# A causal convolution before a gated feed-forward layer: convolution lanes that divide one flat row of chunks and tokens

## The chip, the cores and the metric

One core of a Trainium2 chip runs the whole kernel. The metric is the device time of one execution in microseconds. Its engines run side by side, each with a queue of its own: TensorE (PE, with its weight loads shown as PEld), VectorE (DVE), ScalarE (ACT), GpSimd (POOL) and SyncE (SP, which here only issues DMAs). An instruction waits for another engine on semaphores.

## The reference: what is computed

`x` is (8, 4096, 192): 8 sequences of 4096 tokens, 192 channels in 8 heads of 24. A softmax over 7 taps per head gives the weights of a causal convolution along the tokens; its output goes through a feed-forward layer with a ReLU gate.

```python
w = softmax(weight, axis=-1)                  # (8 heads, 7 taps)
x_pad = concatenate([zeros(B, 6, D), x], axis=1)
conv[b, s, h, g] = sum_k w[h, k] * x_pad[b, s + k, h, g]
xc = conv.reshape(32768, 192)
gate = maximum(xc @ moe_w_gate, 0.0)          # 192 -> 1536
val = xc @ moe_w_val
out = (gate * val) @ moe_w_out                # 1536 -> 192
```

## The kernel before, in words

**Units.** The work is cut into 16 units (`NUNIT`) of 1024 tokens (`UNIT`), each for a pair of sequences at once: `bp` and `bp + 4` are the two streams. A partition holds one channel of one stream: 64 channels of stream 0 on partitions 0 to 63, the same of stream 1 on 64 to 127. The 192 channels make three chunks (`NCH` = 3), so the convolved input of a unit, `xc[u]`, is a tile of 128 partitions x 3 chunks x 1024 tokens.

**Gate phase.** `gate_val(u, w)` (two windows `w` of 512 tokens, 12 blocks `f` of 128 hidden channels each) does 12 matmuls per block into two PSUM tiles (line 450), six for the gate and six for the value; ScalarE takes the ReLU of the gate (line 459), and DVE multiplies it with the value, read straight from PSUM (line 460), into `hT`. PSUM has four tiles `ps`, handed out in turn to everything.

**Projection.** After both windows, three calls of `project_columns(hs, p)` (line 470, 96 matmuls each) make 64 output columns each in a `ps` tile, and `turn_out` (line 484, DVE) transposes each into the output tile. The next unit's gate phase needs the same PSUM tiles: its first gate tile, first value tile and second gate tile are free early, and its second value tile is the one that the third `turn_out` of the unit before releases. `store` then puts four DMAs on SP.

**Convolution lanes.** The first two units are convolved by TensorE (`conv_dense`, `conv`). For all later units `u + 2`, the convolution is done by the other engines while unit `u` is in its projection:

- `lane_load` (GpSimd) loads `x` as `x_e`, tokens on partitions; `lane_turn` copies it on GpSimd into `x_p` (line 375) and turns it by DMA transposes on SP (line 378) into `x_r`, channels on partitions, tokens along the row. `x_r` has nine blocks of 128 (`TILES`): four for DVE's tokens and five for the others', each part with its own 64 tokens of halo ahead of it.
- Of every chunk, DVE has the first 448 tokens (`LDVE`), ScalarE and GpSimd the last 576 (`LPOOL`).
- DVE's part: ScalarE makes tap 0 (`lane_first`, line 416, three instructions), and DVE adds taps 1 to 6 by `scalar_tensor_tensor` (`lane_rest`, line 427): 18 instructions, one per tap and chunk. `STEPS` says how many of them are issued ahead of each of the three `turn_out`s: 5, 6 and 7.
- The other part: ScalarE makes the products of taps 0 to 4 in fp32 (`product`, line 396, 15 instructions), in the order of `TAPS`: taps 1 and 2 in the first third of the projection, 3 and 4 in the second, 0 in the last. GpSimd sums them with `add` (line 405): `prod0 += prod1`, then 2, and so on; taps 5 and 6 (`ON_POOL`) it multiplies itself first (line 398). The last `add` writes `xc`.

**Order on GpSimd.** In the loop over `u`, GpSimd's queue holds `add(u+1, 1)`, `lane_turn(u+2)` and `lane_load(u+3)`, the adds of taps 2 to 5, and the add of tap 6, which is written behind the gate phase in the code but waits for nothing in it. For u = 1 the load and two adds come ahead of `lane_turn`; from u = 13 on there is no load, and at u = 14 no `lane_turn`. Each product tile, `prod0` to `prod6`, has one buffer: a product of the next unit waits until the add that reads that tile is done. `x_r` has two buffers. Nothing is reordered by a planner: the order of each queue is the order in the code.

Of the kernel before, what the change touches and what calls it, by code (L numbers as in the profile page):

```python
# [8 lines left out]
FP = mybir.dt.float32  # L9
F16 = mybir.dt.float16  # L10
ACTF = mybir.ActivationFunctionType
ALU = mybir.AluOpType
# [3 lines left out]
def kernel(  # L16
# [12 lines left out]
    nc = tc.nc  # L29

    B, S, D = x.shape
    H, KW = weight.shape
# [3 lines left out]
    NB = B // 2  # L36
    NCH = D // 64
# [2 lines left out]
    WIN = 512  # L40
    NWIN = S // WIN
    SUB = 112
    ON_POOL = (5, 6)
    STEPS = [5, 6, 7]
    TAPS = [(1, 2), (3, 4), (0,)]
    GSUB = 5


    UNIT = 2 * WIN
    NUNIT = NB * S // UNIT  # L50
    HALO = 64
    LDVE, LPOOL = 448, 576
    TILES = (UNIT + 2 * HALO) // 128
    TDVE = (LDVE + HALO) // 128
    GROUPS = [(0, [WIN * w + SUB * j for j in range(GSUB)]) for w in range(2)]
    second = [min(t, 2 * UNIT - SUB) for t in range(UNIT, 2 * UNIT, SUB)]
    GROUPS += [(0, second[:GSUB]), (0, second[GSUB:])]
# [2 lines left out]
    const = ctx.enter_context(tc.tile_pool(name="const", bufs=1))  # L60
    epool = ctx.enter_context(tc.tile_pool(name="epool", bufs=1))
    rpool = ctx.enter_context(tc.tile_pool(name="rpool", bufs=2))
    apool = ctx.enter_context(tc.tile_pool(name="apool", bufs=1))
# [48 lines left out]
    for half, eng in ((0, nc.sync), (1, nc.scalar)):  # L112
        eng.dma_start(
            out=wr[64 * half : 64 * half + 64],
            in_=bass.AP(
                tensor=weight.tensor,
                offset=weight.offset + 2 * half * HQ * KW,
                ap=[[HQ * KW, 2], [0, 32], [1, HQ * KW]],
            ),
# [79 lines left out]
    tap = const.tile([128, NCH, KW], FP)  # L199

    def load_taps():
# [19 lines left out]
    prod = const.tile([128, HQ, BW, KW], FP)  # L221
# [12 lines left out]
    for q in range(4):  # L234
        for j in range(4):
            s0 = 32 * j - PAD
            lo, hi = max(0, -s0), min(BW, SUB - s0)
# [12 lines left out]
    xc = {}  # L250
# [91 lines left out]
    xes, xrs, accs, prods = {}, {}, {}, {}  # L342

    def lane_load(u):


        bp, t0 = u * UNIT // S, u * UNIT % S
        xe = epool.tile([128, TILES, 2, NCH, 64], F16, name="x_e")
        j0 = int(t0 == 0)
        if j0:  # L350
            nc.gpsimd.memset(xe[0:HALO, 0, :, :, :], 0.0)
        for st in range(2):
            b = bp + NB * st
            for j, n in ((j0, TDVE - j0), (TDVE, TILES - TDVE)):
                lo = t0 - HALO + 128 * j if j < TDVE else t0 + LDVE - HALO
                nc.gpsimd.dma_start(  # L356
                    out=xe[:, j : j + n, st, :, :].rearrange("p j c r -> p j (c r)"),
                    in_=bass.AP(
                        tensor=x.tensor,
                        offset=x.offset + (b * S + lo) * D,  # L360
                        ap=[[D, 128], [128 * D, n], [1, D]],
                    ),
                )
            if j0:
                nc.gpsimd.dma_start(
                    out=xe[HALO:128, 0, st, :, :].rearrange("p c r -> p (c r)"),
                    in_=x[b, 0 : 128 - HALO, :],
                )
        xes[u] = xe

    def lane_turn(u):
        xe = xes.pop(u)
        xp = epool.tile([128, TILES, NCH, 2, 64], F16, name="x_p")
        for st in range(2):
            nc.gpsimd.tensor_copy(out=xp[:, :, :, st, :], in_=xe[:, :, st, :, :])  # L375
        xr = rpool.tile([128, NCH, 128 * TILES], F16, name="x_r")
        for j in range(TILES):
            nc.sync.dma_start_transpose(
                out=xr[:, :, 128 * j : 128 * j + 128],
                in_=xp[:, j].rearrange("p c s r -> p (c s r)"),  # L380
            )
        xrs[u] = xr

    def shifted(u, c, k, lane):
        o = HALO - KW + 1 + k
        if lane:
            return xrs[u][:, c, 128 * TDVE + o : 128 * TDVE + o + LPOOL]
        return xrs[u][:, c, o : o + LDVE]

    def product(engine, u, c, k):  # L390
        if (u, k) not in prods:
            prods[u, k] = apool.tile([128, NCH, LPOOL], FP, name=f"prod{k}")
        out = prods[u, k][:, c, :]
        in_, scale = shifted(u, c, k, 1), tap[:, c, k : k + 1]
        if engine is nc.scalar:
            engine.activation(out=out, in_=in_, func=ACTF.Copy, scale=scale)  # L396
        else:
            engine.tensor_scalar(out=out, in0=in_, scalar1=scale, scalar2=None, op0=ALU.mult)  # L398

    def add(u, k):  # L400
        if k in ON_POOL:
            for c in range(NCH):
                product(nc.gpsimd, u, c, k)
        p0 = prods[u, 0]
        nc.gpsimd.tensor_tensor(  # L405
            out=p0[:] if k < KW - 1 else xc[u][:, :, LDVE:UNIT],
            in0=p0[:],
            in1=prods.pop((u, k))[:],
            op=ALU.add,
        )  # L410

    def lane_first(u):
        accs[u] = apool.tile([128, NCH, LDVE], FP, name="acc")
        xc[u] = xcpool.tile([128, NCH, UNIT], F16, name="xc")
        for c in range(NCH):
            nc.scalar.activation(  # L416
                out=accs[u][:, c, :],
                in_=shifted(u, c, 0, 0),
                func=ACTF.Copy,
                scale=tap[:, c, 0:1],  # L420
            )

    def lane_rest(u):
        acc = accs.pop(u)
        for k in range(1, KW):
            for c in range(NCH):
                nc.vector.scalar_tensor_tensor(  # L427
                    out=xc[u][:, c, 0:LDVE] if k == KW - 1 else acc[:, c, :],
                    in0=shifted(u, c, k, 0),
                    scalar=tap[:, c, k : k + 1],  # L430
                    in1=acc[:, c, :],
                    op0=ALU.mult,
                    op1=ALU.add,
                )
                yield
# [45 lines left out]
    def turn_out(ps, o, p):  # L481


        nc.vector.transpose(  # L484
            out=o[:, :, 64 * p : 64 * p + 64].rearrange("p t (b c) -> p b t c", b=2),
            in_=ps[:].rearrange("p b (t c) -> p b t c", c=32),
        )

    def store(o, bp, w0):
        for s in range(4):  # L490
            row0 = (bp + NB * (s % 2)) * S + WIN * (w0 + s // 2)
            nc.sync.dma_start(
                out=out[row0 : row0 + WIN, :].rearrange("(t p) d -> p t d", p=32),
                in_=o[32 * s : 32 * s + 32],
            )
# [33 lines left out]
    for u in range(NUNIT):  # L529
        lane = 1 <= u < NUNIT - 1  # L530
        if lane:
            add(u + 1, 1)
        if u == 1:
            lane_load(3)
            add(2, 2)
            add(2, 3)
        if u + 2 < NUNIT:
            lane_turn(u + 2)
        if u == 0:
            xts[3] = load_x(3)  # L540
# [12 lines left out]
        bp, w0 = u * UNIT // S, u * UNIT % S // WIN  # L553
        lane = None
        if u + 2 < NUNIT:
            lane_first(u + 2)
            lane = lane_rest(u + 2)
        o = opool.tile([128, UNIT // 64, D], FP, name="out_s")
        if u == NUNIT - 1:
            for i in range(4):  # L560
                project(bp, w0 + i // 2, hs[i // 2], i % 2, i == 3, o[:, 4 * i : 4 * i + 4, :])
            continue
        for p in range(3):
            ps = project_columns(hs, p)
            if lane:
                for k in TAPS[p]:
                    for c in range(NCH):
                        product(nc.scalar, u + 2, c, k)
                for _ in range(STEPS[p]):
                    next(lane)  # L570
            turn_out(ps, o, p)
            if u == 0 and p == 0:
                conv(3)
        store(o, bp, w0)
# [30 lines left out]
```

## Time and profile before

| | |
|---|---|
| Median of 3 runs | 903.69 us (902.73 to 904.63) |
| The profiled execution | 903.87 us, of which the span is 902.2 us |
| PE busy / idle ahead of line 450's value matmuls | 789.6 us / 105.4 us |
| DVE busy | 792.2 us: gate products (line 460) 468.3, lanes (line 427) 214.8 + 50.9, transposes (line 484) 56.1 |
| ACT busy | 568.9 us: ReLU (line 459) 393.2, products (line 396) 141.4, first tap (line 416) 24.9 |
| POOL busy | 597.4 us: adds (line 405) 271.7 + 53.8, products (line 398) 144.3, copies (line 375) 54.3 |
| Granted TensorE clock, mean | 0.934 of full |

Rows of the groups read: line, engine, operation, output<-inputs, shapes, count | busy us, mean ns of one | idle time of the engine just ahead of them, and who ended most of it. Rows of the timeline read: start in us from the span's start, duration in us, engine, line, what, count of merged neighbours, and in brackets the idle time ahead and who ended it; a merged row lasts from its first start to its last end. Matmuls overlap, so a row of six lasts a little longer than the distance to the next row.

### The profile page before, as it was taken

The page shows a single profiled execution, that of the slowest core. Times are in us where ns is not written, and L with a number is a line of the kernel's source. Part 1 is how long each engine was busy: PE and PEld are TensorE (multiplying, and loading weights), DVE is VectorE, ACT ScalarE, POOL GpSimd, SP SyncE. Part 2 cuts the span into 40 slices and gives each one's busy share as a digit, 9 for nine tenths or more (in the row PEclk, how much of TensorE's full clock was granted, in tenths as well). Part 3 has the DMA queues.
Part 4 walks back from the last instruction along what each step waited for, and adds up shares of the span by engine and source line. Part 5 has one row for each costly group of instructions (what it writes and reads, how often), then busy time and mean ns, then how long its engine had stood idle before and what let it go on. Part 6 is the DMA issues. An engine that isn't in the chain of part 4 may idle for free.

```text
span 902.2 us, 21815 instructions
## 1 busy us (share of the span) xinstructions
PE 789.6 (88%) x9392; PEld 402.2 (45%) x9392; DVE 792.2 (88%) x711; ACT 568.9 (63%) x663; POOL 597.4 (66%) x299
## 2 busy tenths in 40 slices
PE   8996979989797997979979798897979929939998
PEld 4543535435353453535435354453535415415447
DVE  7888999989899898998989899898998998989492
ACT  5784847758376684847758477583856807717272
POOL 9429769495894949769396794949849396293000
PEclk9997989989899898989989899898999969969999
DMA  9929434070520707125060340806217004020122
GB/s 113 127 49 143 45 51 100 2 138 13 103 48 4 145 3 121 30 28 123 3 130 20 61 88 1 145 7 110 42 12 140 1 15 96 2 57 14 25 48 71
DMA packets 132580, 55.80 MB, mean 62 GB/s; under 512 B 98180, under 2 KB 132484, under 8 KB 132484
## 3 DMA queue, kind: packets, MB, share of 16 engines
q1 hardware_dynamic: 90466, 38.35, 19.4%
q0 software_dynamic: 41808, 15.97, 16.1%
q8 instruction: 73, 1.20, 0.6%
q14 instruction: 23, 0.19, 0.1%
q10 hardware_dynamic: 210, 0.10, 0.0%
HBM read 31.93 MB, written 25.17 MB: 63 GB/s over the span
## 4 chain that ended last, share of the span: by engine, by line
PE 75%; DVE 19%; issue 4%; DMA 0%; ACT 0%; DVEq 0%
PE ps L450 55%; PE ps L470 18%; DVE acc L427 11%; DVE xc L427 4%; DVE out_s L484 4%; PE ps L506 2%; DMA wr<-in_weight_dram 0%; DVE hT L460 0%; ACT gr L459 0%; PE ps L305 0%; PE ps L280 0%; DVE band L243 0%; DVE prod L224 0%; DVE blk L232 0%; ACT out_s L517 0%
## 5 line engine op out<-in xcount | busy, mean ns | idle before, releaser
L459 ACT ACTIVATE gr<-ps 128x1024 f16<-128x1024 f32 x384 | 393.2, 1024 | 309.8 <-PE ps L450 309.8
L460 DVE TENSOR_TENSOR hT<-gr,ps 128x1024 f16<-128x1024 f16 x384 | 468.3, 1220 | 59.7 <-PE ps L450 26.4
L450 PE MATMUL ps<-xc,Wv 64*128 64x512 f16 x2304 | 334.4, 393 | 105.4 <-DVE out_s L484 103.9
L405 POOL TENSOR_TENSOR prod<-prod,prod 128x1728 f32<-128x1728 f32 x70 | 271.7, 3881 | 212.1 <-ACT prod L396 208.7
L450 PE MATMUL ps<-xc,Wg 64*128 64x512 f16 x2304 | 327.2, 386 | 0.2 <-DVE hT L460 0.2
L450 PEld LDWEIGHTS <-Wv 64*128 64x128 f16 x2304 | 139.0, 97 | 230.9 <-issue 125.1
L470 PE MATMUL ps<-hT,Wo 128*32 128x512 f16 x4320 | 236.0, 379 | 0.0
L427 DVE SCALAR_TENSOR_TENSOR acc<-x_r,tap,acc 128x448 f32<-128x448 f16 x210 | 214.8, 1089 | 1.6 <-ACT acc L416 1.6
L450 PEld LDWEIGHTS <-Wg 64*128 64x128 f16 x2304 | 127.6, 97 | 136.6 <-issue 24.1
L470 PEld LDWEIGHTS <-Wo 128*32 128x32 f16 x4320 | 114.1, 97 | 120.3 <-issue 6.3
L398 POOL TENSOR_SCALAR prod<-x_r,tap 128x576 f32<-128x576 f16 x84 | 144.3, 1731 | 0.0
L396 ACT ACTIVATE prod<-x_r,tap 128x576 f32<-128x576 f16 x210 | 141.4, 765 | 0.0
L484 DVE STREAM_TRANSPOSE out_s<-ps 128x1024 f32<-128x1024 f32 x45 | 56.1, 1246 | 27.0 <-PE ps L470 27.0
L375 POOL COPY x_p<-x_e 128x1728 f16<-128x1728 f16 x28 | 54.3, 1961 | 3.6 <-DMA x_e<-in_x_dram 3.6
L405 POOL TENSOR_TENSOR xc<-prod,prod 128x1728 f16<-128x1728 f32 x14 | 53.8, 3842 | 1.2
L427 DVE SCALAR_TENSOR_TENSOR xc<-x_r,tap,acc 128x448 f16<-128x448 f16 x42 | 50.9, 1263 | 0.0
L356 POOL DMA_DIRECT2D x_e<-in_x_dram x56 | 46.5, 845 | 3.5 <-POOL x_p L375 2.4
L416 ACT ACTIVATE acc<-x_r,tap 128x448 f32<-128x448 f16 x42 | 24.9, 658 | 0.0
L506 PE MATMUL ps<-Wo,hT 128*128 128x192 f16 x192 | 16.0, 246 | 0.0
L506 PEld LDWEIGHTS <-hT 128*128 128x128 f16 x192 | 15.8, 98 | 0.4 <-issue 0.4
L517 DVE COPY out_s<-ps 128x192 f32<-128x192 f32 x1 | 0.4, 358 | 13.3 <-PE ps L506 13.3
L517 ACT COPY out_s<-ps 128x768 f32<-128x768 f32 (+2 forms) x5 | 3.2, 639 | 12.7 <-PE ps L506 12.7
(43 smaller groups left out, 64.3 us busy)
## 6 DMA issues: line engine op xcount, KB each, us to landing
out_dram<-out_s SPq DMA_DIRECT2D x63, 384.0 KB
x_e<-in_x_dram POOLq DMA_DIRECT2D x28, 240.0 KB, 5.9
x_e<-in_x_dram POOLq DMA_DIRECT2D x22, 192.0 KB, 4.7
x_r<-x_p SPq DMA_TRANSPOSE x126
out_s<-in_x_dram POOLq DMA_DIRECT2D x4, 240.0 KB, 6.4
x_e<-in_x_dram POOLq DMA_DIRECT2D x6, 144.0 KB, 5.0
out_s<-in_x_dram POOLq DMA_DIRECT2D x4, 192.0 KB, 4.9
Wo<-in_moe_w_out_dram POOLq DMA_DIRECT2D x1, 576.0 KB, 9.2
```

Source lines behind the costliest of these rows:

```text
L356: nc.gpsimd.dma_start(out=xe[:, j : j + n, st, :, :].rearrange("p j c r -> p j (c r)"), in_=bass.AP(tensor=x.tensor, offset=x.offset + (b ...
L375: nc.gpsimd.tensor_copy(out=xp[:, :, :, st, :], in_=xe[:, :, st, :, :])
L396: engine.activation(out=out, in_=in_, func=ACTF.Copy, scale=scale)
L398: engine.tensor_scalar(out=out, in0=in_, scalar1=scale, scalar2=None, op0=ALU.mult)
L405: nc.gpsimd.tensor_tensor(out=p0[:] if k < KW - 1 else xc[u][:, :, LDVE:UNIT], in0=p0[:], in1=prods.pop((u, k))[:], op=ALU.add,)
L427: nc.vector.scalar_tensor_tensor(out=xc[u][:, c, 0:LDVE] if k == KW - 1 else acc[:, c, :], in0=shifted(u, c, k, 0), scalar=tap[:, c, k : k ...
L450: nc.tensor.matmul(out=pss[i][:, st, :], lhsT=W[64 * st : 64 * st + 64, c, 128 * f : 128 * (f + 1)], rhs=xcb[64 * st : 64 * st + 64, c, WI ...
L459: nc.scalar.activation(out=gr[:], in_=pss[0][:], func=ACTF.Relu)
L460: nc.vector.tensor_tensor(out=h[:, f], in0=gr[:], in1=pss[1][:], op=ALU.mult)
L470: nc.tensor.matmul(out=ps[32 * s : 32 * s + 32, b, :], lhsT=Wo[:, f, 64 * p + 32 * b : 64 * p + 32 * b + 32], rhs=hs[s // 2][:, f, s % 2, ...
L484: nc.vector.transpose(out=o[:, :, 64 * p : 64 * p + 64].rearrange("p t (b c) -> p b t c", b=2), in_=ps[:].rearrange("p b (t c) -> p b t c" ...
L506: nc.tensor.matmul(out=ps[:, i // 2, D * (i % 2) : D * (i % 2) + D], lhsT=h[:, f, st, 128 * q : 128 * (q + 1)], rhs=Wo[:, f, :], start=(f ...
```

## The change

The 3 x 1024 columns of a unit are taken as one flat row of 3072, and the two lanes divide that row instead of each chunk. DVE has the first 1408 columns (`LDVE`): all of chunk 0 and 384 of chunk 1. ScalarE and GpSimd have the other 1664: 640 of chunk 1 and all of chunk 2. A tap still needs its own scale per chunk, so `pieces` cuts each part at the chunk border: two instructions per tap for DVE (1024 and 384 columns), two for ScalarE (640 and 1024). All seven products of that part are now made by ScalarE, in the order 6, 5, 4 | 3, 2 | 1, 0; GpSimd only adds. `STEPS` becomes 3, 4, 5, of 12 instructions. `x_r` is one run of 16 + 1024 tokens per chunk: eight transposes instead of nine, and the 16 tokens of halo are zeroed at the start of a sequence, copied by GpSimd from the end of the unit before, or, for unit 2, loaded and turned apart (`head`, `turned`). `lane_load` has two DMAs instead of four or more.

```diff
-    ON_POOL = (5, 6)
-    STEPS = [5, 6, 7]
-    TAPS = [(1, 2), (3, 4), (0,)]
+    STEPS = [3, 4, 5]
+    TAPS = [(6, 5, 4), (3, 2), (1, 0)]
...
-    HALO = 64
-    LDVE, LPOOL = 448, 576
-    TILES = (UNIT + 2 * HALO) // 128
-    TDVE = (LDVE + HALO) // 128
+    HALO = 16
+    FLAT = NCH * UNIT
+    LDVE = 1408
+    TILES = UNIT // 128
...
+        head = None
+        if t0 and u - 1 not in xes and u - 1 not in xrs:
+            head = const.tile([HALO, 2, NCH, 64], F16, name="head")
+            nc.gpsimd.dma_start(
...
     def lane_turn(u):
-        xe = xes.pop(u)
+        xe, head = xes.pop(u)
+        xr = rpool.tile([128, NCH, HALO + UNIT], F16, name="x_r")
+        if u * UNIT % S == 0:
+            nc.gpsimd.memset(xr[:, :, 0:HALO], 0.0)
+        elif head is None:
+            nc.gpsimd.tensor_copy(out=xr[:, :, 0:HALO], in_=xrs[u - 1][:, :, UNIT : UNIT + HALO])
+        else:
+            turned = const.tile([HALO, NCH, 2, 64], F16, name="turned")
+            for st in range(2):
+                nc.gpsimd.tensor_copy(out=turned[:, :, st, :], in_=head[:, st, :, :])
+            nc.sync.dma_start_transpose(
+                out=xr[:, :, 0:HALO], in_=turned[:].rearrange("p c s r -> p (c s r)")
+            )
...
         for j in range(TILES):
             nc.sync.dma_start_transpose(
-                out=xr[:, :, 128 * j : 128 * j + 128],
+                out=xr[:, :, HALO + 128 * j : HALO + 128 * j + 128],
...
+    def pieces(lo, hi):
+        while lo < hi:
+            c, t = lo // UNIT, lo % UNIT
+            n = min(UNIT - t, hi - lo)
+            yield lo, n, c, t
+            lo += n
...
+    def product(u, k):
+        prods[u, k] = apool.tile([128, FLAT - LDVE], FP, name=f"prod{k}")
+        for at, n, c, t in pieces(LDVE, FLAT):
+            nc.scalar.activation(
+                out=prods[u, k][:, at - LDVE : at - LDVE + n],
+                in_=shifted(u, c, k, t, n),
+                func=ACTF.Copy,
+                scale=tap[:, c, k : k + 1],
+            )
 
     def add(u, k):
-        if k in ON_POOL:
-            for c in range(NCH):
-                product(nc.gpsimd, u, c, k)
         p0 = prods[u, 0]
         nc.gpsimd.tensor_tensor(
-            out=p0[:] if k < KW - 1 else xc[u][:, :, LDVE:UNIT],
+            out=p0[:] if k < KW - 1 else flat(u)[:, LDVE:FLAT],
...
     def lane_rest(u):
         acc = accs.pop(u)
         for k in range(1, KW):
-            for c in range(NCH):
+            for at, n, c, t in pieces(0, LDVE):
                 nc.vector.scalar_tensor_tensor(
-                    out=xc[u][:, c, 0:LDVE] if k == KW - 1 else acc[:, c, :],
-                    in0=shifted(u, c, k, 0),
+                    out=(flat(u) if k == KW - 1 else acc)[:, at : at + n],
+                    in0=shifted(u, c, k, t, n),
                     scalar=tap[:, c, k : k + 1],
-                    in1=acc[:, c, :],
+                    in1=acc[:, at : at + n],
...
                 for k in TAPS[p]:
-                    for c in range(NCH):
-                        product(nc.scalar, u + 2, c, k)
+                    product(u + 2, k)
```

More of the change, by code (lines that the diff above doesn't have):

```diff
@@ L348, in lane_load @@
         xe = epool.tile([128, TILES, 2, NCH, 64], F16, name="x_e")
-        j0 = int(t0 == 0)
-        if j0:
-            nc.gpsimd.memset(xe[0:HALO, 0, :, :, :], 0.0)
         for st in range(2):
[L353 to L368, printed above, removed]
@@ L369, in lane_load @@
-        xes[u] = xe
-    def lane_turn(u):
-        xe = xes.pop(u)
+            row = (bp + NB * st) * S + t0
+            nc.gpsimd.dma_start(
+                out=xe[:, :, st, :, :].rearrange("p j c r -> p j (c r)"),
+                in_=bass.AP(
+                    tensor=x.tensor,
+                    offset=x.offset + row * D,
+                    ap=[[D, 128], [128 * D, TILES], [1, D]],
+                ),
+            )
+        head = None
+        if t0 and u - 1 not in xes and u - 1 not in xrs:
+            head = const.tile([HALO, 2, NCH, 64], F16, name="head")
+            nc.gpsimd.dma_start(
+                out=head[:].rearrange("p s c r -> p s (c r)"),
+                in_=bass.AP(
+                    tensor=x.tensor,
+                    offset=x.offset + (bp * S + t0 - HALO) * D,
+                    ap=[[D, HALO], [NB * S * D, 2], [1, D]],
+                ),
+            )
@@ new lines, in lane_load @@
+        xes[u] = xe, head
+    def lane_turn(u):
+        xe, head = xes.pop(u)
[10 more added lines that the diff above has]
+                out=xr[:, :, 0:HALO], in_=turned[:].rearrange("p c s r -> p (c s r)")
+            )
@@ L375, in lane_turn @@
             nc.gpsimd.tensor_copy(out=xp[:, :, :, st, :], in_=xe[:, :, st, :, :])
-        xr = rpool.tile([128, NCH, 128 * TILES], F16, name="x_r")
         for j in range(TILES):
             nc.sync.dma_start_transpose(
-                out=xr[:, :, 128 * j : 128 * j + 128],
+                out=xr[:, :, HALO + 128 * j : HALO + 128 * j + 128],
                 in_=xp[:, j].rearrange("p c s r -> p (c s r)"),
@@ L382, in lane_turn, with shifted, flat @@
         xrs[u] = xr
[L384 to L398, printed above, removed]
+    def pieces(lo, hi):
[4 more added lines that the diff above has]
+            lo += n
+    def shifted(u, c, k, t, n):
+        o = HALO - KW + 1 + k + t
+        return xrs[u][:, c, o : o + n]
+    def flat(u):
+        return xc[u][:].rearrange("p c t -> p (c t)")
+    def product(u, k):
[6 more added lines that the diff above has]
+                scale=tap[:, c, k : k + 1],
+            )
     def add(u, k):
-        if k in ON_POOL:
-            for c in range(NCH):
-                product(nc.gpsimd, u, c, k)
         p0 = prods[u, 0]
         nc.gpsimd.tensor_tensor(
-            out=p0[:] if k < KW - 1 else xc[u][:, :, LDVE:UNIT],
+            out=p0[:] if k < KW - 1 else flat(u)[:, LDVE:FLAT],
             in0=p0[:],
@@ L412, in lane_first @@
     def lane_first(u):
-        accs[u] = apool.tile([128, NCH, LDVE], FP, name="acc")
+        accs[u] = apool.tile([128, LDVE], FP, name="acc")
         xc[u] = xcpool.tile([128, NCH, UNIT], F16, name="xc")
-        for c in range(NCH):
+        for at, n, c, t in pieces(0, LDVE):
             nc.scalar.activation(
-                out=accs[u][:, c, :],
-                in_=shifted(u, c, 0, 0),
+                out=accs[u][:, at : at + n],
+                in_=shifted(u, c, 0, t, n),
                 func=ACTF.Copy,
@@ L425, in lane_rest @@
         for k in range(1, KW):
-            for c in range(NCH):
+            for at, n, c, t in pieces(0, LDVE):
                 nc.vector.scalar_tensor_tensor(
-                    out=xc[u][:, c, 0:LDVE] if k == KW - 1 else acc[:, c, :],
-                    in0=shifted(u, c, k, 0),
+                    out=(flat(u) if k == KW - 1 else acc)[:, at : at + n],
+                    in0=shifted(u, c, k, t, n),
                     scalar=tap[:, c, k : k + 1],
-                    in1=acc[:, c, :],
+                    in1=acc[:, at : at + n],
                     op0=ALU.mult,
@@ L566 @@
                 for k in TAPS[p]:
-                    for c in range(NCH):
-                        product(nc.scalar, u + 2, c, k)
+                    product(u + 2, k)
                 for _ in range(STEPS[p]):
```

## The prediction, made before the changed kernel had run

> **What bounds the kernel now.** The page first: the busy times, and the group of instructions with the costliest idle time before it.
>
> ```profile
> PE 789.6 (88%) x9392; PEld 402.2 (45%) x9392; DVE 792.2 (88%) x711; ACT 568.9 (63%) x663; POOL 597.4 (66%) x299
> L450 PE MATMUL ps<-xc,Wv 64*128 64x512 f16 x2304 | 334.4, 393 | 105.4 <-DVE out_s L484 103.9
> ```
>
> TensorE sets the pace, except for 103.9 us in which its gate matmuls wait for DVE to transpose the projection out of PSUM. Where that falls is in the timeline of one unit, by engine (unit 6; its projection starts at P = 379.75; times below as P+...).
>
> ```profile
> 379.75 15.72 PE L470 MATMUL ps<-hT,Wo 128*32 128x512 f16 x288
> 396.71 0.81 PE L450 MATMUL ps<-xc,Wg 64*128 64x512 f16 x6
> 403.31 1.47 PE L450 MATMUL ps<-xc,Wv 64*128 64x512 f16 x6 [5.79 <-DVE out_s L484]
> 407.06 0.82 PE L450 MATMUL ps<-xc,Wg 64*128 64x512 f16 x6
> 411.60 0.61 PE L450 MATMUL ps<-xc,Wv 64*128 64x512 f16 x4
> ...
> 330.55 1.25 DVE L484 STREAM_TRANSPOSE out_s<-ps 128x1024 f32<-128x1024 f32 x1 [0.70 <-PE ps L470]
> ...
> 381.40 3.06 DVE L427 SCALAR_TENSOR_TENSOR acc<-x_r,tap,acc 128x448 f32<-128x448 f16 x5
> 385.16 1.25 DVE L484 STREAM_TRANSPOSE out_s<-ps 128x1024 f32<-128x1024 f32 x1 [0.70 <-PE ps L470]
> 386.33 3.62 DVE L427 SCALAR_TENSOR_TENSOR acc<-x_r,tap,acc 128x448 f32<-128x448 f16 x6
> 390.34 1.25 DVE L484 STREAM_TRANSPOSE out_s<-ps 128x1024 f32<-128x1024 f32 x1 [0.38 <-PE ps L470]
> 391.51 8.79 DVE L427 SCALAR_TENSOR_TENSOR acc<-x_r,tap,acc 128x448 f32<-128x448 f16 x4
> 400.23 1.86 DVE L427 SCALAR_TENSOR_TENSOR xc<-x_r,tap,acc 128x448 f16<-128x448 f16 x3
> 402.02 1.24 DVE L484 STREAM_TRANSPOSE out_s<-ps 128x1024 f32<-128x1024 f32 x1
> ...
> 392.04 3.87 POOL L405 TENSOR_TENSOR prod<-prod,prod 128x1728 f32<-128x1728 f32 x1 [13.45 <-ACT prod L396]
> 395.85 3.99 POOL L375 COPY x_p<-x_e 128x1728 f16<-128x1728 f16 x2
> ...
> 380.13 1.77 ACT L416 ACTIVATE acc<-x_r,tap 128x448 f32<-128x448 f16 x3
> 381.80 10.09 ACT L396 ACTIVATE prod<-x_r,tap 128x576 f32<-128x576 f16 x15
> ```
>
> Eleven lane instructions run at 0.60 us each. Then ScalarE's last product ends (391.89), GpSimd's first add starts (392.04), and four take 8.79 us. Line 427 in that stretch, minimum, median and maximum in ns:
>
> ```profile
> L427 DVE SCALAR_TENSOR_TENSOR acc<-x_r,tap,acc x4: 644/2038/4311, 391.5 to 398.3; 128x448 f32<-128x448 f16 x4
> ```
>
> One is free, one lasts 4.31 (the 3.87 add and its own 0.45), two 2.04 (one GpSimd copy each). So one lane instruction gets through per GpSimd instruction: each engine waits out the other's instruction. The same at both ends of the kernel (units 0, 12, 13):
>
> ```profile
> 59.86 2.43 DVE L427 SCALAR_TENSOR_TENSOR acc<-x_r,tap,acc 128x448 f32<-128x448 f16 x4
> 62.20 11.94 DVE L427 SCALAR_TENSOR_TENSOR xc<-x_r,tap,acc 128x448 f16<-128x448 f16 x3
> ...
> 62.44 4.15 POOL L405 TENSOR_TENSOR prod<-prod,prod 128x1728 f32<-128x1728 f32 x1 [26.64 <-ACT prod L396]
> ...
> 727.92 12.56 DVE L427 SCALAR_TENSOR_TENSOR xc<-x_r,tap,acc 128x448 f16<-128x448 f16 x3
> 784.29 13.20 DVE L427 SCALAR_TENSOR_TENSOR acc<-x_r,tap,acc 128x448 f32<-128x448 f16 x4
> ```
>
> The add that came at 62.44 during an instruction took 4.15, 0.3 more than elsewhere: it waited, and went ahead of the next one. So the wait in each unit is set by **when GpSimd's adds begin while lane instructions remain**, not by how many columns DVE has.
>
> **The cycle.** Transposes at 330.55 and 385.16: 54.61 us per unit. TensorE's work at full clock is 48 groups of six at 0.649 ((411.60-407.06)/7) and 15.65 of projection (to 395.40, two groups before 396.71), 46.8. It runs dry at 396.71+0.65 = P+17.6 and resumes at P+23.56: 5.95 idle. The rest, 1.8, is three groups at half clock until 407.06. The clock, by stretches (us, busy PE, PEld, DVE, ACT, POOL, granted clock, DMA):
>
> ```profile
> 396.80:400.20 3.40, 0.72 (x8) 0.20 (x5) 3.40 (x2) 1.51 (x2) 3.10 (x3) 1.00 0.00 0
> 400.20:403.60 3.40, 0.29 (x2) 0.13 (x3) 3.40 (x6) 0.00 (x0) 3.40 (x5) 0.50 0.67 67
> 403.60:407.00 3.40, 3.40 (x18) 1.42 (x16) 1.99 (x2) 0.91 (x1) 3.40 (x1) 0.50 1.31 147
> 789.30:792.70 3.40, 0.99 (x10) 0.35 (x7) 3.40 (x1) 1.78 (x2) 3.40 (x1) 1.00 0.00 0
> 792.70:809.80 17.10, 5.27 (x26) 2.24 (x27) 15.24 (x9) 1.02 (x1) 16.86 (x7) 0.50 0.23 48
> ```
>
> Half clock lasts 6.8 and 17.1 us, 2 and 5 times 3.41, and the cycle is 16 times 3.41: the clock is judged in steps of 3.41, and a step with PE busy 0.72 or 0.99 of 3.40 is followed by half clock.
>
> **The change, part by part.** GpSimd loses six products per unit (they go to ScalarE), DVE gets 1408 columns per tap in pieces of 1024 and 384 instead of three of 448, ScalarE 14 products of 1024 and 640.
>
> ```profile
> L396 ACT ACTIVATE prod<-x_r,tap 128x576 f32<-128x576 f16 x210 | 141.4, 765 | 0.0
> L416 ACT ACTIVATE acc<-x_r,tap 128x448 f32<-128x448 f16 x42 | 24.9, 658 | 0.0
> L405 POOL TENSOR_TENSOR prod<-prod,prod 128x1728 f32<-128x1728 f32 x70 | 271.7, 3881 | 212.1 <-ACT prod L396 208.7
> L375 POOL COPY x_p<-x_e 128x1728 f16<-128x1728 f16 x28 | 54.3, 1961 | 3.6 <-DMA x_e<-in_x_dram 3.6
> L356 POOL DMA_DIRECT2D x_e<-in_x_dram x56 | 46.5, 845 | 3.5 <-POOL x_p L375 2.4
> ```
>
> *ScalarE.* 107 ns for 128 elements is 0.836 per element, so 384, 640, 1024 take 0.60, 0.82, 1.14. Neighbours overlap by 0.10 (15 x 0.765 against 10.09). Seven taps of 1.96, the first tap's 1.74, less 15 overlaps: 13.96 instead of 11.76. It ends at P+0.38+13.96 = P+14.34, and GpSimd's first add, which needs taps 1 and 0, the last two, comes 0.15 later, **P+14.49 instead of P+12.29**.
>
> *DVE.* No 1024-wide lane instruction is in the trace. From 0.60 per 448 it lies between 0.60 (all fixed) and 1.38 (all per element). The nearest row is the 1024-wide transpose, 1.25, its follower 1.17 after its start; I take 1.20, and 0.53 for 384. Parts one and two of the projection then need 2.9 and 3.5 us, and still wait for TensorE (0.70 and 0.38 now), so their saving is worth nothing. Part three starts at P+11.76 with 384, 1024, 384, 1024, 384: starts at P+11.76, 12.29, 13.49, 14.02, 15.22. **GpSimd comes at 14.49, in the fourth.** It waits until 15.2, adds for 3.70 (3.84 free, by 1664/1728) until 18.9, and only the last, short piece waits behind it, done at 19.3. Its transpose starts as it ends, TensorE resumes 1.29 later (402.02 to 403.31): P+20.54, idle 2.9 instead of 5.95. With 1.38 for the long piece the fourth starts at 14.16, still ahead of GpSimd, and TensorE resumes at 20.6; with 0.60 for all the last starts at 14.2 and is free (rival A).
>
> The Trainium skill, "Vector Engine (DVE) Microarchitecture Reference", section 7, speaks against this: a scalar_tensor_tensor with two SBUF sources that aren't bf16 runs at half rate. An estimate by that page and the 0.96 GHz of "VectorE: DVE Perf Modes" is 0.93 us for 448 and 2.13 for 1024, which would be rival B. The trace disagrees: 0.60.
>
> *GpSimd after that* works under the gate phase, where DVE's products read one SBUF operand and ran unhindered beside its adds: the halo copy (no such row; above nothing and below the 1.96 of a copy 36 times as wide, 0.3 taken), two copies (at most 1.96), two DMA issues instead of four (0.85 each), five adds: done by P+43. "Last taps first" makes ScalarE's first product wait for the very last add (tap 6's buffer); it asks at P+53, so 10 us hide it. Were they gone, taps, adds and the relus queued behind them would slip one for one.
>
> *The moved x_r.* Eight transposes instead of nine behind the stores on SP:
>
> ```profile
> 406.89 16.73 SPq L378 DMA_TRANSPOSE x_r<-x_p  x9
> 80.99 15.04 SPq L378 DMA_TRANSPOSE x_r<-x_p  x9
> ```
>
> They now start at about P+24 and take 8 x 1.86, ready by P+41 for P+51. Unit 2's extra head DMA, two tiny copies and a transpose replace its ninth transpose. Unit 3's start at 81 and end about 95, when they are needed.
>
> *Unit 0*, on TensorE:
>
> ```profile
> 65.05 0.81 PE L450 MATMUL ps<-xc,Wg 64*128 64x512 f16 x6
> 75.35 1.46 PE L450 MATMUL ps<-xc,Wv 64*128 64x512 f16 x6 [9.49 <-DVE out_s L484]
> ```
>
> GpSimd comes 2.2 later than the 62.44 above, at 64.6; DVE's last five start at 59.86 and need 4.0, 63.9: nothing waits. Transposed by 65.2, before TensorE runs dry at 65.70; 45 groups on, unit 1's projection starts at **94.9**.
>
> *The sum.* A cycle is 46.8+2.9 = 49.7 at full clock, and 1.7 more (half of a step) where a step counts as idle: 51.4. Locked to 15 steps it is 51.2, which needs a step with 1.0 of 3.4 busy to count as idle, the edge of what the rows show. I take 51.0 for units 2 to 13, and 49 for unit 1, where a late x_r may delay GpSimd past DVE (47) or not (51). Units 12 and 13 become ordinary. The end is unchanged:
>
> ```profile
> 841.77 1.25 DVE L484 STREAM_TRANSPOSE out_s<-ps 128x1024 f32<-128x1024 f32 x1 [3.68 <-PE ps L470]
> ```
>
> Unit 14's projection starts 5.41 earlier, at 836.4; from there 65.8. Span 94.9+49+12x51.0+65.8 = 821.7; the profiled execution took 903.87 for a span of 902.2, so 1.7 outside: **823**. Its 903.87 stands 0.02% over the median of 903.69.
>
> **The rivals.**
> - **The clock stays full (14%).** If only a whole empty step lowers it, an idle of 2.9 never does: 49.7 a cycle, 808. Against it: 0.72 and 0.99 busy were followed by half clock. The Trainium skill, "TensorE: Matmul & The Clock Gate", part 1, says half clock comes after an idle window of about 3.4 us; here the windows agree in length, and fall though not empty.
> - **A, nothing waits (11%).** If GpSimd comes 0.73 later, or DVE's third part is 0.73 quicker, the last piece goes first, and TensorE never runs dry: 13 cycles of 46.9, 772.
> - **B, two wait (12%).** If DVE's third part is 0.47 slower, the add goes ahead of the long piece too, and GpSimd's next copy ahead of the last: TensorE resumes at P+21 to 22.8, cycles of 51.4 to 53.8, 828 to 858. The bound of 1.38 uses 0.14 of that 0.47.
> - **C, slower than before (7%).** x_r's rows are now 2080 bytes and begin 32 bytes in, where all began at multiples of 256. A cycle can't be shorter than P+24, eight transposes and their landing (1.5 assumed), less the 0.4 until ScalarE asks: 25.2+8t. At today's t of 1.86 that is 40; from 3.25 it decides, and above 4.0 the mean cycle passes the 57.0 that 13 cycles may have to equal 902. At 4.1: about 916. Against it: the two rows above have 1.67 and 1.86, and 3.25 is far off.
> - **No effect (2%).** If long lane instructions come from something that stays, such as the third part's place, 904.
>
> **Chances and range.** Forecast 54%, own range 813 to 831 (cycles of 50.3 to 51.4, unit 1 47 to 51). With the full clock and B that is 80%: 798 to 858. Faster by over 0.2% (about what a measurement here tells from none) 54+14+11+12 = 91%, within 2%, slower 7%.
>
> **What would show it.** GpSimd's first add some 14.5 us after a projection starts, in a 1024-wide lane instruction; one lane instruction per unit of over 3 us, a 384-wide one; TensorE's wait for line 484's successor near 3 us in 12 or 13 units, none in unit 0; cycles at 51.2 or between 49.7 and 51.4. Two long ones mean B, none A. The forecast falls if x_r's transposes take over 3 us, or ScalarE stands before tap 6.

## The result, and the profile after

| | before | changed |
|---|---|---|
| Median | 903.93 us (902.73 to 904.63, 4 runs) | 828.89 us (827.73 to 829.98, 4 runs) |
| Ratio | 1 | 0.9171, 95% interval 0.9155 to 0.9187 |
| Profiled execution, and its span | 903.87, 902.2 | 829.14, 827.4 |
| Granted TensorE clock, mean | 0.934 | 0.973 |

The forecast was 823 us with a range of 798 to 858, and 813 to 831 for its own case. One of the four executions of the run act_all below took 2819.72 us; its time and ratio go by the other three.

The page of the changed kernel first: busy times, the idle group that bounded the kernel before, and GpSimd's adds, each the counterpart of a row shown above (lines 450, 484, 427, 405 of before are 468, 502, 445, 423 now).

```profile
PE 784.5 (95%) x9392; PEld 401.2 (48%) x9392; DVE 720.7 (87%) x627; ACT 599.2 (72%) x635; POOL 414.8 (50%) x194
L468 PE MATMUL ps<-xc,Wv 64*128 64x512 f16 x2304 | 329.4, 388 | 36.1 <-DVE out_s L502 34.9
L423 POOL TENSOR_TENSOR prod<-prod,prod 128x1664 f32<-128x1664 f32 x70 | 267.6, 3823 | 320.6 <-ACT prod L414 317.1
```

TensorE's wait for the transposes has fallen from 103.9 to 34.9 us. The timeline of the same unit (6), whose projection now starts at P = 351.70, by engine:

```profile
351.70 15.72 PE L488 MATMUL ps<-hT,Wo 128*32 128x512 f16 x288
368.67 0.81 PE L468 MATMUL ps<-xc,Wg 64*128 64x512 f16 x6
372.16 1.46 PE L468 MATMUL ps<-xc,Wv 64*128 64x512 f16 x6 [2.69 <-DVE out_s L502]
375.61 0.82 PE L468 MATMUL ps<-xc,Wg 64*128 64x512 f16 x6
...
353.36 3.00 DVE L445 SCALAR_TENSOR_TENSOR acc<-x_r,tap,acc 128x1024 f32<-128x1024 f16 x3
357.12 1.25 DVE L502 STREAM_TRANSPOSE out_s<-ps 128x1024 f32<-128x1024 f32 x1 [0.76 <-PE ps L488]
363.48 2.30 DVE L445 SCALAR_TENSOR_TENSOR acc<-x_r,tap,acc 128x384 f32<-128x384 f16 x3
365.69 5.25 DVE L445 SCALAR_TENSOR_TENSOR xc<-x_r,tap,acc 128x1024 f16<-128x1024 f16 x2
370.87 1.24 DVE L502 STREAM_TRANSPOSE out_s<-ps 128x1024 f32<-128x1024 f32 x1
...
366.18 4.35 POOL L423 TENSOR_TENSOR prod<-prod,prod 128x1664 f32<-128x1664 f32 x1 [22.78 <-ACT prod L414]
370.48 0.55 POOL L377 COPY x_r<-x_r 128x48 f16<-128x48 f16 x1
...
352.08 1.65 ACT L434 ACTIVATE acc<-x_r,tap 128x1024 f32<-128x1024 f16 x2
353.63 12.41 ACT L414 ACTIVATE prod<-x_r,tap 128x640 f32<-128x640 f16 x14
```

Line 445 in the third part of that projection, minimum, median and maximum in ns:

```profile
L445 DVE SCALAR_TENSOR_TENSOR acc<-x_r,tap,acc x3: 575/610/1277, 363.5 to 365.2; 128x384 f32<-128x384 f16 x2, 128x1024 f32<-128x1024 f16 x1
L445 DVE SCALAR_TENSOR_TENSOR xc<-x_r,tap,acc x2: 1278/2668/4058, 365.7 to 366.9; 128x1024 f16<-128x1024 f16 x1, 128x384 f16<-128x384 f16 x1
```

One lane instruction is long, 4.06 us, and it is the short one of 384 columns. GpSimd's add came at 366.18, inside the 1024-wide one before it, lasted 4.35 instead of some 3.7 (it waited), and the last piece waited for the add. Before, three were long, 8.4 us together. In the changed kernel TensorE waits 2.68 or 2.69 us in 13 units, and not at all in unit 0, where the first add comes after the last lane instruction.

Where the 74.8 us of span went is read from the first transpose of a projection (5.41 after its start in both kernels), of units 1 and 12 before, and 1, 2, 12 and 14 after:

```profile
111.96 1.25 DVE L484 STREAM_TRANSPOSE out_s<-ps 128x1024 f32<-128x1024 f32 x1 [0.70 <-PE ps L470]
712.85 1.25 DVE L484 STREAM_TRANSPOSE out_s<-ps 128x1024 f32<-128x1024 f32 x1 [0.69 <-PE ps L470]
```

```profile
100.75 1.25 DVE L502 STREAM_TRANSPOSE out_s<-ps 128x1024 f32<-128x1024 f32 x1 [0.52 <-PE ps L488]
152.14 1.25 DVE L502 STREAM_TRANSPOSE out_s<-ps 128x1024 f32<-128x1024 f32 x1 [0.76 <-PE ps L488]
664.33 1.25 DVE L502 STREAM_TRANSPOSE out_s<-ps 128x1024 f32<-128x1024 f32 x1 [0.76 <-PE ps L488]
766.73 1.25 DVE L502 STREAM_TRANSPOSE out_s<-ps 128x1024 f32<-128x1024 f32 x1 [3.68 <-PE ps L488]
```

Up to unit 1, 11.2 us; units 1 to 11, 600.89 against 563.58, 37.3; units 12 and 13, 128.92 against 102.40, 26.5. The rest is the end, 0.2 longer.

### The profile page after: what moved, and what is told of

Same layout as the page of the kernel before. It is cut to its first block, busy times and chain, and to the rows that moved or that the text cites. A ratio compares the mean times of both kernels' runs of the same rounds, so it can differ in the third digit from the quotient of the medians.

```text
span 827.4 us, 21544 instructions
## 1 busy us (share of the span) xinstructions
PE 784.5 (95%) x9392; PEld 401.2 (48%) x9392; DVE 720.7 (87%) x627; ACT 599.2 (72%) x635; POOL 414.8 (50%) x194
## 4 chain that ended last, share of the span: by engine, by line
PE 82%; DVE 13%; issue 3%; DMA 1%; ACT 0%; DVEq 0%
PE ps L468 59%; PE ps L488 20%; DVE xc L445 5%; DVE out_s L502 4%; DVE acc L445 3%; PE ps L524 2%; DMA wr<-in_weight_dram 1%; DVE hT L478 0%; ACT gr L477 0%; PE ps L304 0%; DVE band L242 0%; DVE prod L223 0%; DVE blk L231 0%; DVE xc L289 0%; DVE Wg L167 0%
## 5 line engine op out<-in xcount | busy, mean ns | idle before, releaser
L478 DVE TENSOR_TENSOR hT<-gr,ps 128x1024 f16<-128x1024 f16 x384 | 468.1, 1220 | 53.3 <-ACT gr L477 19.0
L423 POOL TENSOR_TENSOR prod<-prod,prod 128x1664 f32<-128x1664 f32 x70 | 267.6, 3823 | 320.6 <-ACT prod L414 317.1
L468 PE MATMUL ps<-xc,Wv 64*128 64x512 f16 x2304 | 329.4, 388 | 36.1 <-DVE out_s L502 34.9
L414 ACT ACTIVATE prod<-x_r,tap 128x640 f32<-128x640 f16 x196 | 173.9, 977 | 0.0
L445 DVE SCALAR_TENSOR_TENSOR acc<-x_r,tap,acc 128x1024 f32<-128x1024 f16 (+1 forms) x140 | 123.3, 939 | 2.3 <-ACT acc L434 2.1
L445 DVE SCALAR_TENSOR_TENSOR xc<-x_r,tap,acc 128x1024 f16<-128x1024 f16 (+1 forms) x28 | 70.1, 2546 | 0.0
L423 POOL TENSOR_TENSOR xc<-prod,prod 128x1664 f16<-128x1664 f32 x14 | 51.9, 3708 | 1.1
L387 POOL COPY x_p<-x_e 128x1536 f16<-128x1536 f16 x28 | 41.0, 1490 | 2.1 <-DMA x_e<-in_x_dram 2.1
L350 POOL DMA_DIRECT2D x_e<-in_x_dram x28 | 25.0, 898 | 3.8 <-POOL x_p L387 3.6
L434 ACT ACTIVATE acc<-x_r,tap 128x1024 f32<-128x1024 f16 (+1 forms) x28 | 23.0, 872 | 0.2 <-issue 0.2
L128 PE MATMUL ps<-zeros 128*128 128x512 f16 x16 | 6.1, 568 | 1.5 <-DVE zeros L125 1.5
```

Of the source, the lines that this page charges most:

```text
L350: nc.gpsimd.dma_start(out=xe[:, :, st, :, :].rearrange("p j c r -> p j (c r)"), in_=bass.AP(tensor=x.tensor, offset=x.offset + row * D, ap ...
L414: nc.scalar.activation(out=prods[u, k][:, at - LDVE : at - LDVE + n], in_=shifted(u, c, k, t, n), func=ACTF.Copy, scale=tap[:, c, k : k + 1],)
L423: nc.gpsimd.tensor_tensor(out=p0[:] if k < KW - 1 else flat(u)[:, LDVE:FLAT], in0=p0[:], in1=prods.pop((u, k))[:], op=ALU.add,)
L434: nc.scalar.activation(out=accs[u][:, at : at + n], in_=shifted(u, c, 0, t, n), func=ACTF.Copy, scale=tap[:, c, 0:1],)
L445: nc.vector.scalar_tensor_tensor(out=(flat(u) if k == KW - 1 else acc)[:, at : at + n], in0=shifted(u, c, k, t, n), scalar=tap[:, c, k : k ...
L468: nc.tensor.matmul(out=pss[i][:, st, :], lhsT=W[64 * st : 64 * st + 64, c, 128 * f : 128 * (f + 1)], rhs=xcb[64 * st : 64 * st + 64, c, WI ...
```

## The experiments

Ten runs, grouped by what they test. Changes are against the changed kernel unless said otherwise; ratios are to the kernel before, with their 95% intervals.

### xr_alone: the one run of x_r with the lanes of before

```diff
-    STEPS = [3, 4, 5]
-    TAPS = [(6, 5, 4), (3, 2), (1, 0)]
+    ON_POOL = (5, 6)
+    STEPS = [5, 6, 7]
+    TAPS = [(1, 2), (3, 4), (0,)]
...
-    LDVE = 1408
+    LDVE, LPOOL = 448, 576
...
```

with `product`, `add`, `lane_first` and `lane_rest` of before.

> Only the one run of x_r (eight transposes, a 16-token halo, the head of unit 2) with the lanes of before: three chunks of 448 and 576, taps 5 and 6 multiplied by GpSimd. Theory (the time is set by which lane instructions of DVE wait behind GpSimd): the moved x_r is hidden, GpSimd's first add comes 12.3 us after a projection starts, four lane instructions take some 9 us, cycles of 54.6: 900 to 905 us. Rival (the single run of x_r, its fewer DMAs and transposes bring part of the 75 us): below 890.

Measured: 947.06 us, ratio 1.0476 (1.0446 to 1.0506). Both expectations miss: this part alone makes the kernel before 43 us slower. In its unit 7, GpSimd and DVE (timeline), and the last three lane instructions:

```profile
479.95 1.84 POOL L350 DMA_DIRECT2D x_e<-in_x_dram  x2 [0.31 <-POOL x_p L387]
481.81 11.95 POOL L416 TENSOR_TENSOR prod<-prod,prod 128x1728 f32<-128x1728 f32 x3
...
478.24 7.90 DVE L438 SCALAR_TENSOR_TENSOR xc<-x_r,tap,acc 128x448 f16<-128x448 f16 x3
...
L438 DVE SCALAR_TENSOR_TENSOR xc<-x_r,tap,acc x3: 673/1877/5503, 478.2 to 480.6; 128x448 f16<-128x448 f16 x3
```

The projection of this unit starts at 459.27. With two DMA issues instead of four, GpSimd's second add comes 22.5 us after it, where it came 23.7 after (unit 6 before, 403.43), and a lane instruction that is still left takes 5.5 us: it gets through only behind that add. Making GpSimd's queue shorter made DVE slower. Why this instruction did not get through ahead of the add's record is taken up in the last section.

### act_all and act_all_again: the kernel before with all products by ScalarE

```diff
-    ON_POOL = (5, 6)
+    ON_POOL = ()
-    TAPS = [(1, 2), (3, 4), (0,)]
+    TAPS = [(1, 2, 3), (4, 5), (6, 0)]
```

(against the kernel before)

> The kernel before with only one edit: taps 5 and 6 are multiplied by ScalarE instead of GpSimd, tap 0 still last. Lanes, instruction counts of DVE (18 per unit) and x_r stay. ScalarE then ends 21 products and the first tap at 0.38 + 15.7 us after the projection's start, GpSimd's first add comes at about 16.3, and the last lane instruction starts at about 15.4: none waits. Theory: cycles of 46.9, TensorE idle under 5 us in all ahead of the value matmuls, 768 to 778 us, faster than the changed kernel though DVE issues half as many instructions more. Rival (the gain comes from fewer and longer lane instructions or from the flat split): between 870 and 904.

Measured: 781.4 us, ratio 0.8636 (0.8619 to 0.8653): 122 us off the kernel before by two lines, with its 18 lane instructions, its lanes per chunk and its x_r. So neither the flat row nor fewer instructions is needed for a gain of this kind, and the two lines alone are 47.5 us faster than the whole change. It is 3 us above its expectation.

> The kernel before with taps 5 and 6 multiplied by ScalarE, for the profile of an ordinary execution. Theory: no lane instruction over 1 us, TensorE's wait ahead of the value matmuls under 5 us in all, cycles of 46.9; the 8 us above 773 then lie in a few places outside the ordinary cycle, the late x_r of unit 3 first. Rival (the lanes still wait behind GpSimd in part of the units): lane instructions of 2 to 4 us, evenly spread.

Measured: 782.51 us in one run. The waits, and the timeline of unit 1, say where the excess lies:

```profile
PE ps L450 <- DVE out_s L484: 7.8, 1, 7.8
...
98.61 1.79 ACT L416 ACTIVATE acc<-x_r,tap 128x448 f32<-128x448 f16 x3 [1.54 <-DMA x_r<-x_p]
...
114.16 6.80 DVE L427 SCALAR_TENSOR_TENSOR xc<-x_r,tap,acc 128x448 f16<-128x448 f16 x3
```

One wait of 7.8 us in the whole kernel, in unit 1, where unit 3's x_r is late (ScalarE waits 1.54 us for it). TensorE waits for the transposes nowhere else, and from unit 2 on every cycle is 46.8 us, as expected. In unit 1 the expectation misses: lane instructions of over 4 us, and a wait above 5.

### first_taps: the products in the other order

```diff
-    TAPS = [(6, 5, 4), (3, 2), (1, 0)]
+    TAPS = [(0, 1, 2), (3, 4), (5, 6)]
```

> The changed kernel with ScalarE's products in the order 0, 1, 2 | 3, 4 | 5, 6, all else the same. GpSimd's first add then comes some 5.7 us after the projection's start, and its instructions run through the second and third part of the projection; seven or eight lane instructions, one per GpSimd instruction, wait. Theory: TensorE resumes 30 to 37 us after the projection's start instead of 20.5, cycles of 60 to 66: 950 to 1040 us, slower than the kernel before. Rival (the order of the taps is without weight, the shape of the lanes makes the time): 825 to 835.

Measured: 1094.07 us, ratio 1.2096 (1.2077 to 1.2115): 265 us over the changed kernel with the same instructions, and above the expected 1040. GpSimd's first add in unit 6, whose projection starts at 401.59, line 445 from there, and TensorE's wait:

```profile
407.27 3.76 POOL L423 TENSOR_TENSOR prod<-prod,prod 128x1664 f32<-128x1664 f32 x1 [39.15 <-ACT prod L414]
...
L445 DVE SCALAR_TENSOR_TENSOR acc<-x_r,tap,acc x7: 1272/3275/4702, 408.2 to 426.0; 128x384 f32<-128x384 f16 x4, 128x1024 f32<-128x1024 f16 x3
L445 DVE SCALAR_TENSOR_TENSOR xc<-x_r,tap,acc x2: 4033/4368/4702, 429.9 to 434.5; 128x1024 f16<-128x1024 f16 x1, 128x384 f16<-128x384 f16 x1
...
439.80 1.46 PE L468 MATMUL ps<-xc,Wv 64*128 64x512 f16 x6 [20.44 <-DVE out_s L502]
```

The add comes 5.7 us after the start, as expected, but all of the nine lane instructions after it but one (the 1.27, a 1024-wide one) are long, and TensorE resumes after 38.2 us, not 30 to 37. Eight waited, as expected; they cost more than was forecast.

### ldve1216 and ldve1280: fewer columns for DVE

```diff
-    LDVE = 1408
+    LDVE = 1216
```

and 1280 in the other.

> The changed kernel with DVE's part of the flat row 1216 columns instead of 1408 (pieces of 1024 and 192; ScalarE and GpSimd 1856). ScalarE ends 0.96 us later, GpSimd's first add comes 15.4 us after the projection's start instead of 14.5, and DVE's last piece starts at 14.8 instead of 15.2, so it is through before. Theory: no lane instruction waits, the clock stays full, cycles of 46.9: 768 to 778 us. Rival (the columns on each engine set the time, ScalarE and GpSimd being given 12% more): 829 or slower.

> The changed kernel with 1280 columns for DVE (pieces of 1024 and 256). GpSimd's first add comes 15.1 us after the projection's start and DVE's last piece starts at 14.95: ahead by about 0.15 us. Theory (who comes first has the port for a whole instruction): no wait, 770 to 778 us, as with 1216; if the estimate of the 0.15 is off, the add goes first in some or all units, up to 830, with nothing in between in any one unit. Rival (the time follows the columns): halfway between 829 and 773, near 792.

Measured: 773.26 us, ratio 0.8553 (0.8539 to 0.8566), and 772.67 us, ratio 0.8548 (0.8536 to 0.8561). Both are faster than the kernel before and the changed one. The rival by columns (829 or slower for 1216, halfway for 1280) falls. With 1280, unit 6's last two lane instructions, GpSimd's first add, and the same two in ns:

```profile
343.79 1.67 DVE L445 SCALAR_TENSOR_TENSOR xc<-x_r,tap,acc 128x1024 f16<-128x1024 f16 x2
345.19 4.11 POOL L423 TENSOR_TENSOR prod<-prod,prod 128x1792 f32<-128x1792 f32 x1 [17.53 <-ACT prod L414]
...
L445 DVE SCALAR_TENSOR_TENSOR xc<-x_r,tap,acc x2: 476/876/1276, 343.8 to 345.0; 128x1024 f16<-128x1024 f16 x1, 128x256 f16<-128x256 f16 x1
```

The last piece starts at 345.0, 0.2 us ahead of the add, and takes 0.48; with 1408 it started 0.7 us after the add and took 4.06. In the kernel of 1216 the granted clock is 1.000 over the whole span, and TensorE is busy nearly throughout:

```profile
PE 762.0 (99%) x9392; PEld 384.6 (50%) x9392; DVE 661.5 (86%) x627; ACT 612.3 (79%) x635; POOL 437.0 (57%) x194
```

### half_add: the first add cut in two

```diff
+        n = FLAT - LDVE
+        cuts = [0, n // 2, n] if k == 1 else [0, n]
+        for lo, hi in zip(cuts, cuts[1:]):
-        nc.gpsimd.tensor_tensor(
-            out=p0[:] if k < KW - 1 else flat(u)[:, LDVE:FLAT],
+            nc.gpsimd.tensor_tensor(
+                out=p0[:, lo:hi] if k < KW - 1 else flat(u)[:, LDVE:FLAT],
...
```

> The changed kernel with GpSimd's first add of each unit cut into two of 832 columns; same work, one instruction more. The last lane instruction then waits behind 1.9 us instead of 3.7, and goes between the halves. Theory: TensorE waits 0.8 to 0.9 us per unit, too little of a step for the clock to fall, so the 1.7 us of half clock go as well: cycles of 47.7, 780 to 788 us. Rivals: the clock falls all the same, 803 to 808; the last lane instruction does not get its turn between two adds, or the wait has another cause, 827 or more.

Measured: 786.6 us, ratio 0.8695 (0.8681 to 0.8709). TensorE's wait and the last two lane instructions of unit 6:

```profile
PE ps L472 <- DVE out_s L506: 12.1, 13, 0.9
...
L449 DVE SCALAR_TENSOR_TENSOR xc<-x_r,tap,acc x2: 1280/1793/2306, 348.9 to 350.1; 128x1024 f16<-128x1024 f16 x1, 128x384 f16<-128x384 f16 x1
```

The long one fell from 4.06 to 2.31 us: it goes between the halves. 13 waits of 0.93 instead of 2.69 are 22.8 us less; the time fell by 42.3. The other 19.5, 1.5 for each of 13 units, is half clock that no longer occurs: the mean clock is 1.000, and TensorE's busy time fell from 784.5 to 764.2 us. So the wait is priced, and so is the clock.

### pad05 and pad10: more work ahead of the third transpose

```diff
+            if lane and p == 2:
+                nc.vector.memset(pad[:], 0.0)
             turn_out(ps, o, p)
```

with a tile `pad` of 448 and of 960 fp32 columns that nothing reads.

> The changed kernel, with 0.53 us more work for DVE (a 448-wide memset of a tile that nothing reads) ahead of the third transpose of each of the 14 units with lanes, so TensorE waits some 3.2 us instead of 2.7. Theory (cycles lock to 15 steps of 3.41 us, because half clock ends on a step's border): TensorE starts later into the step of half clock and loses less there; cycles stay at 51.2 and the time within 0.3% of 829: 827 to 832 us. Rival (waits add up): 13 or 14 times 0.53 more, 835 to 837. If a step with some 40% busy no longer counts as idle, the lock breaks and cycles lie between 50.0 and 51.7.

> The same with 1.06 us (960-wide): TensorE waits some 3.75 us. Theory of the lock: 51.2 again, 827 to 833 us, if a step with 55% busy still counts as idle; if not, cycles of 50.6 to 52.3 that wander, 820 to 843. Rival (waits add up): 842 to 844.

Measured: 839.42 us, ratio 0.9284 (0.9268 to 0.9299), and 847.8 us, ratio 0.9374 (0.9342 to 0.9406). Every time expected of pad05 misses: the wait grew by only 0.41 (3.10 us in each of 13 units, against 2.69), 5.3 us in all, and the time by 10.5. TensorE's waits, pad05 and then pad10:

```profile
PE ps L469 <- DVE out_s L503: 40.3, 13, 3.1
...
PE ps L469 <- DVE out_s L503: 44.0, 14, 3.6
```

The clock by steps (us, busy PE, PEld, DVE, ACT, POOL, granted clock, DMA), three of the changed kernel, then four of pad05 around a wait of its unit 3:

```profile
368.50:371.90 3.40, 0.98 (x10) 0.34 (x7) 3.40 (x2) 1.77 (x2) 3.40 (x3) 0.99 0.00 0
371.90:375.30 3.40, 3.14 (x16) 1.35 (x17) 2.54 (x3) 0.36 (x1) 3.10 (x4) 0.51 0.56 125
375.30:378.70 3.40, 3.40 (x36) 1.69 (x31) 2.39 (x2) 2.62 (x3) 3.39 (x2) 1.00 0.82 168
```

```profile
215.00:218.30 3.30, 1.14 (x12) 0.39 (x7) 3.26 (x3) 1.93 (x2) 3.30 (x3) 1.00 0.00 0
218.30:221.70 3.40, 2.46 (x12) 1.01 (x13) 2.88 (x3) 0.00 (x0) 3.10 (x3) 0.50 0.39 88
221.70:225.10 3.40, 3.40 (x18) 1.41 (x16) 1.56 (x2) 1.54 (x2) 3.39 (x3) 0.50 0.81 145
225.10:228.00 2.90, 2.90 (x30) 1.45 (x28) 1.92 (x2) 1.99 (x3) 2.82 (x2) 0.99 1.18 174
```

The step that follows the fall was busy for 3.14 of 3.40 in the changed kernel, and the clock came back; in pad05 it was busy for 2.46, and half clock lasted a second step, 1.7 us more. That undoes the lock to 15 steps: a later start inside the slow step doesn't merely lose less, it can buy a whole second slow step. It does so in three of the 13 units (3, 7 and 11), whose cycles are 53.0 to 53.1 us, where the others are 51.45 to 51.81; 13 x 0.41 and 3 x 1.7 make 10.4 of the 10.5 us. pad10 lies above every range given for it as well. In its profiled execution (844.96 us) TensorE waits 3.63 us in units 2 to 13, and their cycles are 52.1 to 52.4 and 53.3 to 53.5 us by turns, close to 31 steps of 3.41 for two: half clock lasts one step and two steps by turns. Its four executions fall into two pairs, 845.0 and 845.4, and 850.3 twice; what parts them is open.

### xr_alone_4dma: what xr_alone had lost

```diff
-            nc.gpsimd.dma_start(
-                out=xe[:, :, st, :, :].rearrange("p j c r -> p j (c r)"),
+            for j in (0, TILES // 2):
+                nc.gpsimd.dma_start(
+                    out=xe[:, j : j + TILES // 2, st, :, :].rearrange("p j c r -> p j (c r)"),
...
```

(against xr_alone)

> The one run of x_r with the lanes of before, as in xr_alone (947 us), but with x_e loaded by four DMAs per unit as before instead of two, so GpSimd's queue has four issues between the copies and the second add again. Theory (what xr_alone lost is that GpSimd's next adds come sooner, while lane instructions remain): the last lane instructions fit beside the four issues, cycles of 54 to 55 throughout, 898 to 908 us. Rival (the shorter row of x_r or its shifted start makes DVE, ScalarE or the transposes slower): 930 or more.

Measured: 901.23 us, ratio 0.997 (0.996 to 0.9979). As expected, the same bytes in four DMAs instead of two are 45.8 us faster, with x_r, transposes and lanes unchanged. Its last three lane instructions, the last two of them beside the issues (unit 7):

```profile
452.50 3.07 DVE L439 SCALAR_TENSOR_TENSOR xc<-x_r,tap,acc 128x448 f16<-128x448 f16 x3
455.29 2.23 POOL L351 DMA_DIRECT2D x_e<-in_x_dram  x3 [0.26 <-issue]
457.52 11.69 POOL L417 TENSOR_TENSOR prod<-prod,prod 128x1728 f32<-128x1728 f32 x3
```

## Why the prediction was right

**What bounds.** That the wait is set by when GpSimd's adds begin while lane instructions remain is shown from both sides: the order of the products alone moves the time from 829 to 1094, a start of the add that lies behind the last lane instruction gives 773 with either 1216 or 1280 columns, and the kernel before gains 122 us when ScalarE takes over GpSimd's products, which makes the add later, without any of the rest. (GpSimd's own products ran in the gate phase, from 360.5 to 374.7 ahead of unit 6's projection at 379.75, when no lane instruction was left.) half_add shows that it is GpSimd's instruction that the lane instruction waits for: when that is cut in half, the lane instruction gets through in the middle.

**ScalarE and GpSimd.** Forecast: GpSimd comes at P+14.49 and is done by P+43. Measured: 366.18, P+14.48, and 394.8, P+43.1.

**DVE.** Forecast 1.20 and 0.53 per piece, the fourth start at P+14.02, one 384-wide piece waiting, TensorE back at P+20.54. Measured: 365.69, P+13.99; one 384-wide piece of 4.06; 372.16, P+20.46. The 1.20 was borrowed from the row of a transpose, and no row beforehand showed that it would fit; the bound of 1.38 would have left the order the same. The 1024-wide instruction takes 1.28 from start to end. The half-rate rule of the Trainium skill's "Vector Engine (DVE) Microarchitecture Reference", section 7, doesn't hold for this form (f16 and f32 inputs, f32 result). An estimate by that rule and the 0.96 GHz of the Trainium skill's page "VectorE: DVE Perf Modes" is at least 2.13 for 1024 columns.

**Parts costed at nothing.** The first two parts of the projection still wait for TensorE (0.76 us ahead of the first transpose, 0.51 ahead of the second), as said. The moved x_r was hidden in the changed kernel, but the cover that was named was the wrong one: the step looked at when the transposes are ready, and not at what the shorter GpSimd queue does to lane instructions that are left. Where several are left, as in xr_alone, it costs 43 us, and four DMA issues in place of two take that back (xr_alone_4dma). In the changed kernel only one is left, and it goes behind the first add.

**The sum.** Unit 1's projection starts at 95.3 (forecast 94.9); unit 1's cycle is 51.4 (49); units 2 to 13 have 614.59/12 = 51.22 (51.0); from unit 14's projection, 761.3, to the end 66.1 (65.8). The 5.7 us between 821.7 and 827.4 are 0.4, 2.4, 2.6 and 0.3. The largest shares are unit 1, where x_r was not late enough to let DVE's last piece through, and the clock: I took 51.0, between a fall in every unit and none.

**The clock.** A fall in every unit and cycles locked to 15 steps of 3.41, 51.2, was the upper edge of the forecast's case, and is what happened: with the wait unchanged, the cycles from unit 1 on are 51.39, 51.30, 51.25 and 51.22 us, and then 51.19 to 51.21. The rival of a clock that stays full fell: 0.98 of 3.40 busy counted as idle, as 0.99 had before. The mechanism of the lock as I used it is wrong in one respect, and pad05 shows it: half clock ends on a border only if the step before was busy enough. It held here since TensorE resumed at 372.16, about 0.2 us behind the border near 371.9.

**The rivals.** A (nothing waits, 772) is what ldve1280 and ldve1216 are: 773. It didn't come for 0.7 us, the margin that the prediction gave as 0.73. B and C didn't come: one instruction waits, not two, and the eight transposes were not what the lanes waited for. They take 1.95 us each, not the 3.25 from which they would decide, and are over at P+40.7:

```profile
376.79 15.57 SPq L389 DMA_TRANSPOSE x_r<-x_p  x8
```

## What to carry to other kernels

Where two engines exclude each other instruction by instruction, the place of the first instruction of the one against the last of the other counts for more than how much work either has: here 0.7 us at that border decided over 56 us (829 to 773). Look for such a border before balancing columns, and test a shortened queue for what it brings forward. A wait of TensorE can cost more than its length: 2.69 us per unit cost 4.4 with the clock (cycles of 51.2 against the 46.8 of ldve1280), and 0.93 cost about its own length (786.6 against 773.3 us, 1.0 for each of 13 units).

## What the runs showed of the hardware that was not expected

- **One lane instruction per GpSimd instruction** is a turn, not a rate. Halving an add (half_add) gave the waiting DVE instruction its turn between the halves, 2.31 us instead of 4.06.
- **The clock comes back by steps too.** After a fall, a step with 2.46 of 3.40 us busy left the clock at half, one with 3.14 restored it. Steps with 0.98 and 1.14 busy were followed by a fall; waits of 0.93 never were. Where between these the borders lie wasn't tried. The Trainium skill, "TensorE: Matmul & The Clock Gate", part 1, gives a window of 3.413 us and an idle window as the condition for half clock. The length fits the steps of 3.41 here; for the condition, a step that is 29% busy (0.98 of 3.40) is enough.
- **A DMA issue on GpSimd is not always room for DVE.** In xr_alone a lane instruction that started at 480.6, during two issues and 1.2 us ahead of the next add's record (481.81), still waited that add out; in xr_alone_4dma three went through in 3.07 us, two of them beside the four issues. Why is open: the records of GpSimd don't show it, and it wasn't tried apart.
